# Two attentions and a gate on one core: the gate's path moved from DRAM to DVE, and the planner's rules for transfers changed

## The chip, the cores and the metric

The kernel runs on one core of a Trainium2 chip. The metric is device time in microseconds, less being better: the median of several runs. A profiled execution is one more run, and the profile's span goes from its first to its last instruction. Engines: TensorE (PE, its weight loads PEld), VectorE (DVE), ScalarE (ACT), GpSimd (POOL) and SyncE (SP), whose queue issues all transfers here.

## The reference

For 2048 tokens of width 640 there are two attentions of 32 heads (20 channels each), A and B, mixed by a gate that each token computes:

```python
g = sigmoid((x * gate_w).sum(-1, keepdims=True))
a = A(x, wq, wk, wv, wo, beta)      # 4 segments of 512 tokens
b = B(x, wqkv, wo)                  # causal window of 256 tokens
return g * a + (1 - g) * b
```

A is causal softmax attention within a segment, plus a memory: `num = phi(q) @ M`, `den = phi(q) @ z`, with `M` and `z` summed over `phi(k)` and `v` of the earlier segments, where `phi(t)` is `t + 1` for positive t and else `exp(t)`. A head's sigmoid of `beta` mixes `num / den` with the softmax part. Inputs and outputs are float32.

## The kernel before, in words

**Tiling.** The work is cut into 16 head groups `T` (four segments s, and in each of them the groups g = 0, 2, 1, 3 of `head(T)`; g below 2 is A, from 2 on B), and each of these into four units `u` of four heads, 64 in all. For a head group the projections run first: five column tiles `m` of q and k (`plan_qk`, matmuls of L432), and four token blocks of v (`plan_v`, L553). They are float32 products made of three matmuls on high and low halves, so each weight tile is loaded (`wst`, `xst`), split by ACT (L381) and by POOL or DVE (L397) into `w` or `wv`, and then used. q and k are split into three bfloat16 parts (`plan_parts`), stored to DRAM (`dq`, `dk`, by `qk_store`) and read back as stacks `qst`, `kst`, one set for each unit (`stack_read`). Likewise phi goes to `dphi` and `dphq` and comes back (`mem_load` into `pks`, `mem_stack` into `qfs`).

**A unit.** It first finds the maximum of each row: matmuls into PSUM (`max_mm`, L644), a reduction on DVE (`max_red`, L655), splits and a transpose (`mrs`, `mt`), two stores to DRAM (`max_store`, L682) and a read of three rows into the unit's own `qst` (`max_rows`, L686). Only then may the scores be computed, with the maximum subtracted in the same matmul (`st_mm`, L709), then the exponential on ACT (L716), masks on POOL (L722, L725), and the product with v (`av_mm`, L739). The result is scaled, transposed and stored (`o_store`), read back for the output projection (`o_load`, L432 with `ohl`) and stored.

**The gate.** The v projection of head group g = 0 has one more column, `gate_w`. `z_out` (L562) copies it to `zg`, one column for each of the segment's four token blocks. `z_store` (L566) writes these 4 x 128 values to DRAM (`dz`), single floats apart, and `z_load` (L570) reads them back into `zc` in the layout of the transposed output, repeated for four groups of 32 partitions. `z_exp` (ACT, L574) and `z_sig` (DVE, L578 to L580) make the sigmoid and one minus it. `fac` and `den_mul` scale by them later.

**What sets the order.** The kernel is written as a list of items: `add(t, engine, duration, function, ...)` with a due time `t` in units, the buffers that it makes (`new`), adds to (`put`), changes (`mod`) or reads (`get`), and for a transfer its size. `Plan.order` then plays a list scheduler: among the items whose dependencies are met it takes the one that can start first, by the due time's order on a tie, and the result is the order in which each engine's instructions are issued. It holds a model of 16 DMA rings: a transfer of `took` us per ring begins when its rings are free and lands `DM` us after them. What the model says of times decides only the order; on the chip the semaphores decide when things run. The tables at the head set due times: `AHEAD` (projections before their units), `RD` (reads of the stacks), `MT` and `MS` (maxima and what follows them), `PACE` (how far a projection may run ahead of the scores).

Of the kernel before, what the change touches and what calls it, by code (L numbers as in the profile page):

```python
# [37 lines left out]
NPX, NMI, NOB = 7, 2, 2  # L38
AHEAD, RD, PACE = 4.26, 2.5, 2.18
TL, OZ, WL = 1.16, 5, 0.006  # L40
P0, MA, DP, NF, NR = 3.97, 0.94, 0.0, 1, 2
MT, MS = 1.3, 0.58
WARM = 26
LM, LR, LA, AT = 0.99, 2.03, 0.0, 0.11
DM, XP, XO, XS = 0.9, 0.32, 0.2, 0.11
OA = {5: 2, 6: 3, 7: 2, 8: 2, 9: 2, 10: 2, 11: 3, 12: 3, 13: 2, 14: 2, 15: 2}
AV = ((0, 1, 2),)
EPS = 1e-6

# [5 lines left out]
class Plan:  # L55
# [38 lines left out]
    def order(self):  # L94
# [7 lines left out]
        for i, (t, _, eng, dur, fn, a, new, mod, put, get, size, pace, cols, _, bank, _, _) in enumerate(items):  # L102
# [48 lines left out]
            for name in get:  # L151
                s = slot(name)
                deps[i] |= set(s["puts"])
# [26 lines left out]
        while len(out) < n:  # L180
            best = None
            for e, c in cand.items():
                cold = e == "pe" and self.cold(free[e])
                for i in c:
                    at = free[e]
                    if e == "pe":
                        at += max(0.0, items[i][13][0] - tail)
                    z = max(at, ready[i]) + (items[i][15] if tail > 0.06 else 0.0)
                    if items[i][16] and e in ("dve", "pool"):
                        z = max(z, port)  # L190
                    if items[i][14]:
# [69 lines left out]
@with_exitstack  # L261
def gated_mix_kernel(ctx: ExitStack, tc: tile.TileContext, xt, wqk, wv, wo, beta, ident, out):
# [6 lines left out]
    attention(ctx, tc, const, dram, xt, wqk, wv, wo, beta, ident, o_dram, out)  # L269


def attention(ctx, tc, const, dram, xt, wqk, wv, wo, beta, ident, o_dram, out):
    nc = tc.nc
# [17 lines left out]

    idf = const.tile([128, 128], F32, name="idf")

    mask_a = const.tile([128, 512], BF16, name="mask_a")
# [60 lines left out]
    zg = const.tile([128, 16], F32, name="zg")  # L355
    dz = [dram.tile([L], F32, name=f"dz{i}") for i in range(NSEG)]
    zc = const.tile([128, 2, 2, 16], F32, name="zc")
# [166 lines left out]
    def plan_qk(t, dt, T, m):  # L524
# [3 lines left out]
        t += NC * dt - 0.01  # L528
        ph, dk = ("phi", T, m), ("dq", T)
        plan_parts(t + 1e-4, k, k)  # L530
        add(t + 3e-4, SP, SI * len(runs_of(m)), qk_store, T, m, put=[dk], get=[("hl", k)], size=3 * 2 ** 17, packet=1024)
        nk = rows_of(m, 1) if g < 2 and s < NSEG - 1 else 0
# [5 lines left out]
        if nk:  # L538
            add(t + 7e-4, SP, SI * len(runs_of(m, (1,))), phi_store, T, m, get=[ph],
                new=[("dphi", 2, ("dphi", T))] if m == 1 else [], put=[("dphi", T)] if m > 1 else [], size=2048 * nk)  # L540
        if nq:
            plan_parts(t + 8e-4, ph, ph)
            add(t + 1e-3, SP, SI * len(runs_of(m, (0,))), phl_store, T, m, get=[("hl", ph)],
                new=[("dphq", 2, ("dphq", T))] if m == 0 else [], put=[("dphq", T)] if m else [], size=3072 * nq, packet=1024)

# [18 lines left out]

    def z_store(s):
        nc.sync.dma_start(bass.AP(tensor=dz[s].tensor, offset=dz[s].offset, ap=[[1, 4], [16, 32], [4, 4]]),  # L566
                          zg[:, 4 * s:4 * s + 4])

    def z_load(s):
        nc.sync.dma_start(zc[:, s % 2, 0], bass.AP(tensor=dz[s].tensor, offset=dz[s].offset,  # L570
                                                   ap=[[0, 4], [16, 32], [1, 16]]))

    def z_exp(s):
        nc.scalar.activation(zc[:, s % 2, 0], zc[:, s % 2, 0], AF.Exp, scale=-1.0)  # L574

    def z_sig(s):
        z = zc[:, s % 2, 0]
        nc.vector.tensor_scalar(z, z, 1.0, None, op0=ALU.add)  # L578
        nc.vector.reciprocal(z, z)
        nc.vector.tensor_scalar(zc[:, s % 2, 1], z, -1.0, 1.0, op0=ALU.mult, op1=ALU.add)  # L580

# [5 lines left out]
    def plan_v(t, dt, T, b):  # L587
# [8 lines left out]
        if g == 0:  # L596
            add(t + 1e-4, DVE, 0.08, z_out, T, b, get=[k], put=["zg"])
            if b == 3:
                add(t + 2e-4, SP, DI, z_store, s, get=["zg"], put=[("dz", s)], size=2048, packet=4)
                add(t + 3e-4, SP, DJ, z_load, s, get=[("dz", s)], new=[("z", 2, ("z", s))], size=8192, packet=64, rings=4)  # L600
                add(t + 4e-4, ACT, 0.25, z_exp, s, mod=[("z", s)])
                add(t + 5e-4, DVE, 0.7, z_sig, s, mod=[("z", s)])

# [340 lines left out]
    add(-25, PE, 0.107 * WARM, c_warm, bank=("warm", 1, "warm"), cols=256 * WARM)  # L944
    add(-16.5, SP, 1.1, c_load, put=["cl"], size=2 ** 16)
    add(-3, ACT, 0.25, c_exp, get=["cl"], put=["ce"])
# [5 lines left out]
    for T in range(NT + 2):  # L952
# [38 lines left out]
        for u in range(4 * T, 4 * T + 4):  # L991
            tr = u - RD
            for i in range(3):
                for w in range(2):
# [16 lines left out]
    for u in range(NU):  # L1011
# [91 lines left out]
def layout(A_x, A_wq, A_wk, A_wv, A_wo, A_beta, B_x, B_wqkv, B_wo, gate_w):  # L1103
# [16 lines left out]
    def turn(w):  # L1120
        return w.reshape(NC, 128, NC, 128).transpose(2, 1, 0, 3).reshape(NC, 128, D)
    return dict(xt=n(n(A_x)[0].T), wqk=n(np.stack([turn(w) for w in qk])), wv=n(np.stack(vv)),
                wo=n(np.stack([turn(w) for w in (n(A_wo)[rows], n(B_wo)[rows], n(B_wo))])),
                beta=n(n(A_beta).reshape(8, 4).T), ident=np.eye(128, dtype=np.float32))

# [14 lines left out]
```

## Time and profile before

| | |
|---|---|
| runs (3) | 1178.53 us median, 1175.38 to 1179.56 |
| the profiled execution | 1183.04 us, its span 1181.3 us |
| mean granted TensorE clock | 0.979 |
| PE busy | 1093.2 us, 93% |
| DVE, ACT, POOL busy | 66%, 60%, 69% |
| transfers | 224.24 MB, mean 190 GB/s |

The profile is read like this: a group's line gives engine, operation, output<-input and shape, then busy time, mean duration and the idle time before it with what ended it (`<-`). A wait's row names who waited, for whom, the sum, the count and the longest, in us. A row of the chain that ended last gives its start, its length and what filled it; where that is a transfer, it runs from the issue to the landing. `SPq` is the queue that issues transfers. Names of buffers are those of the kernel, without numbers.

### The profile page before, as it was taken

To read this page: it belongs to the slowest core of one execution; us is meant where nothing else is said; L and a number is where in the kernel's file an instruction comes from. 1 tells how busy PE (TensorE), PEld (TensorE's weight loads), DVE (VectorE), ACT (ScalarE), POOL (GpSimd) and SP (SyncE) were. 2 spreads that over 40 slices of the span, in tenths; PEclk is the share of its full clock that TensorE was granted. 3 is DMA by queue.
4 is the path that set the end of the run, shared out by engine and by line. 5 is a ranking of instruction groups with operands and counts; after the bars stand their busy time and mean duration, and the time that the engine had idled before them with its cause. 6 is when DMAs were issued, how large, how long until landed. Compare 5 with 4: busy or idle time off the path is not lost.

```text
span 1181.3 us, 25003 instructions
## 1 busy us (share of the span) xinstructions
PE 1093.2 (93%) x8322; PEld 718.9 (61%) x8322; DVE 778.6 (66%) x2640; ACT 704.6 (60%) x1496; POOL 816.1 (69%) x1063
## 2 busy tenths in 40 slices
PE   9789999997999999989798999997979899999996
PEld 7565666664556666656465666665646557665564
DVE  3477887665768667976666866676647577567711
ACT  6246756675467755567454776646636477645661
POOL 9436674786568776688655877667757587756874
PEclk9989999998999999999899999999999999999999
DMA  6868878778887599777787868887588676788423
GB/s 212 171 180 195 220 195 206 186 192 183 218 204 197 143 210 253 200 193 219 160 219 188 204 167 220 209 209 178 156 171 223 172 206 160 220 202 216 137 91 107
DMA packets 194753, 224.24 MB, mean 190 GB/s; under 512 B 80768, under 2 KB 143616, under 8 KB 194624
## 3 DMA queue, kind: packets, MB, share of 16 engines
q1 hardware_dynamic: 194624, 222.64, 73.9%
q8 instruction: 66, 1.08, 0.4%
q14 instruction: 63, 0.52, 0.2%
HBM read 157.62 MB, written 64.95 MB: 188 GB/s over the span
## 4 chain that ended last, share of the span: by engine, by line
PE 52%; DMA 29%; DVE 6%; POOL 5%; ACT 3%; SPq 3%; issue 2%; POOLq 0%; DVEq 0%; ACTq 0%
PE bank L432 19%; PE bank L709 9%; PE bank L553 8%; PE bank L739 8%; PE bank L644 8%; DMA qst<-dmx 5%; DMA dmx<-mt 5%; DMA qst<-dq 4%; DMA xst<-wv 3%; DMA kst<-dk 3%; DVE bank L655 3%; DMA wst<-wqk 2%; DMA xst<-o_dram 2%; ACT P L716 1%; DMA pks<-dphi 1%
## 5 line engine op out<-in xcount | busy, mean ns | idle before, releaser
L716 ACT ACTIVATE P<-bank 128x512 f32<-128x512 f32 (+2 forms) x768 | 374.1, 559 | 121.6 <-PE bank L709 101.2
L432 PE MATMUL bank<-xhl,w 128*128 128x512 f32 x1200 | 363.8, 429 | 1.4 <-DVE xhl L397 0.4
L655 DVE CUSTOM_DVE_ANT_0 bank<-bank,mask_b 128x384 f32<-128x384 f32 (+2 forms) x512 | 260.2, 549 | 65.0 <-PE bank L644 63.9
L644 PE MATMUL bank<-kst,qst 120*128 120x384 bf16 (+3 forms) x1024 | 258.9, 314 | 33.8 <-DVE mx L655 12.8
L655 DVE CUSTOM_DVE_ANT_0 bank<-bank,mask_a 128x128 f32<-128x128 f32 (+3 forms) x512 | 238.2, 511 | 74.9 <-PE bank L644 73.6
L709 PE MATMUL bank<-qst,kst 123*128 123x384 bf16 (+2 forms) x1216 | 231.8, 293 | 38.6 <-DMA qst<-dmx 29.8
L397 POOL TENSOR_TENSOR w<-wst,w 128x640 fp32r<-128x640 f32 x119 | 185.4, 1558 | 92.5 <-ACT w L381 92.2
L432 PEld LDWEIGHTS bank<-xhl,w 128*128 128x128 f32 x1200 | 218.9, 192 | 46.1 <-issue 1.9
L722 POOL TENSOR_SCALAR_AFFINE_SELECT P<-P 128x512 f32<-128x512 f32 x256 | 161.0, 636 | 86.1 <-ACT P L716 80.2
L553 PE MATMUL bank<-wv,xhl 128*128 128x320 f32 (+1 forms) x960 | 194.9, 337 | 0.7 <-POOL wv L397 0.2
L432 PE MATMUL bank<-ohl,w 128*128 128x512 f32 x600 | 178.8, 425 | 6.5 <-POOL w L397 2.7
L709 PEld LDWEIGHTS <-kst 123*128 123x128 bf16 x1216 | 91.9, 99 | 142.3 <-issue 70.8
L644 PEld LDWEIGHTS <-qst 120*128 120x128 bf16 x1024 | 82.9, 99 | 131.1 <-issue 94.6
L739 PE MATMUL bank<-P,vau 128*32 128x384 f32 (+3 forms) x2432 | 159.9, 407 | 1.2 <-DVE mt L789 0.8
L553 PEld LDWEIGHTS bank<-wv,xhl 128*128 128x128 f32 x960 | 153.7, 192 | 11.4 <-DVE mx L655 1.4
L655 DVE DVE_READ_ACCUMULATOR2_ANT mx<- 128x1 f32 x1024 | 143.2, 140 | 0.0
L451 POOL TENSOR_TENSOR hl<-res,hl 128x512 bf16<-128x512 f32 x104 | 121.1, 1166 | 23.7 <-ACT hl L381 19.9
L820 DVE STREAM_TRANSPOSE ot<-bank 128x512 f32<-128x512 f32 x88 | 62.7, 713 | 108.5 <-PE bank L739 98.1
L432 PEld LDWEIGHTS bank<-ohl,w 128*128 128x128 f32 x600 | 109.4, 191 | 31.9 <-POOL ohl L397 4.6
L739 PEld LDWEIGHTS bank<-P,vau 128*32 128x32 f32 x2432 | 69.0, 109 | 82.3 <-issue 66.4
L381 ACT ACTIVATE w<-wst 128x640 fp32r<-128x640 f32 x121 | 89.5, 741 | 40.8 <-PE bank L432 16.3
L397 POOL TENSOR_TENSOR wv<-xst,wv 128x322 fp32r<-128x322 f32 x79 | 68.6, 878 | 48.6 <-ACT wv L381 46.7
(73 smaller groups left out, 907.9 us busy)
## 6 DMA issues: line engine op xcount, KB each, us to landing
wst<-wqk SPq DMA_DIRECT2D x80, 320.0 KB
o_dram<-ot SPq DMA_DIRECT2D x64, 256.0 KB
qst<-dq SPq DMA_DIRECT2D x64, 240.0 KB
kst<-dk SPq DMA_DIRECT2D x64, 240.0 KB
wst<-wo SPq DMA_DIRECT2D x41, 320.0 KB
xst<-wv SPq DMA_DIRECT2D x80, 161.0 KB
qst<-dq SPq DMA_DIRECT2D x64, 192.0 KB
xst<-o_dram SPq DMA_DIRECT2D x35, 256.0 KB
```

The costliest lines, as they stand in the source:

```text
L381: nc.scalar.activation(dst, src, AF.Copy)
L397: EN[e].tensor_tensor(out=t[:, 1], in0=B.pop(src), in1=f(t[:, 0]), op=ALU.subtract)
L432: nc.tensor.matmul(p, w[:, a, col:col + 128], x[:, b], start=(c == 0 and i == 0), stop=(c == NC - 1 and i == 2))
L451: EN[e].tensor_tensor(out=t[:, LO], in0=B["res", k], in1=t[:, MI], op=ALU.subtract)
L553: nc.tensor.matmul(p[:, :n], x[:, a, 128 * b:128 * b + 128], w[:, bb, :n], start=(c == 0 and i == 0), stop=(c == NC - 1 and i == 2))
L644: nc.tensor.matmul(pt[:, :n], qst[u % NQ][0:6 * DH, h, 128 * b:128 * b + 128], keys(u, 6 * DH, h, c0, n), start=True, stop=True)
L655: nc.vector.tensor_tensor_reduce(out=x, in0=x, in1=mk, scale=1.0, scalar=BIG, op0=ALU.add, op1=ALU.max, accum_out=B["M", u][:, j:j + 1])
L709: nc.tensor.matmul(pt[:, c:c + 128 * n], keys(u, 6 * DH + 3, h, c0, 128), q[0:6 * DH + 3, h, 128 * q0:128 * (q0 + n)], start=True, stop=True)
L716: nc.scalar.activation(B["P", u, b][:, 2 * p + r, c0:c1], B["st", u, b, p, r][:, c0:c1], AF.Exp, scale=SCALE)
L722: nc.gpsimd.affine_select(out=v, in_=v, pattern=[[0, 4], [1, 128]], compare_op=ALU.is_ge, fill=0.0, base=0, channel_multiplier=-1)
L739: nc.tensor.matmul(o[32 * j:32 * j + 32, 128 * q0:128 * (q0 + n)], v[:, VA * h:VA * h + 32], t[:, j, c:c + 128 * n], start=(b == 0 and i = ...
L820: nc.vector.transpose(B["ot", u][:, i].rearrange("p b e -> p (b e)"), B["o" if i == 0 else "num", u])
```

## The change

Five things:

- The gate no longer goes through DRAM. `z_move` copies `zg` by DVE, for each of four groups of 32 partitions, into the first 32 partitions of `zc`; exponential and sigmoid run on 32 partitions, and three more copies repeat the result.
- In the planner a transfer that takes more than `BULK` = 0.3 us on a ring is not planned to start until its rings have less than `BACK` = 3 us of work left. The maxima's stores and reads are shorter than that.
- `DM`, the planned time from the end of a transfer to its landing, is 1.5 instead of 0.9; the due times of projections, stacks and maxima are earlier (`AHEAD` 4.7, `RD` 2.9, `MT` 1.5, `MS` 0.78), and `PACE` is 2.6.
- Units 0 and 1 of a head group wait for the first half of q, k and phi, units 2 and 3 for the second, where each waited for what was declared of the whole.
- An identity matrix that nothing used is no longer loaded.

```diff
-AHEAD, RD, PACE = 4.26, 2.5, 2.18
+AHEAD, RD, PACE = 4.7, 2.9, 2.6
-MT, MS = 1.3, 0.58
+MT, MS = 1.5, 0.78
-DM, XP, XO, XS = 0.9, 0.32, 0.2, 0.11
+DM, XP, XO, XS = 1.5, 0.32, 0.2, 0.11
+BACK, BULK = 3, 0.3
...
+                    if items[i][10] and items[i][10][0] > BULK:
+                        z = max(z, max(dma[:items[i][10][1]]) - BACK)
...
     def c_load():
-        nc.sync.dma_start(idf, ident)
...
+        def halves(tag, kind):
+            first = lambda du: min(z for z in range(NC) for r in runs_of(z, (kind,)) if r[0] == du)
+            du = sorted({z[0] for z in runs_of(m, (kind,))})
+            return dict(new=[((tag, z), 2, (tag, T, z)) for z in du if first(z) == m],
+                        put=[(tag, T, z) for z in du if first(z) != m])
...
-    def z_store(s):
-        nc.sync.dma_start(bass.AP(tensor=dz[s].tensor, offset=dz[s].offset, ap=[[1, 4], [16, 32], [4, 4]]),
-                          zg[:, 4 * s:4 * s + 4])
-
-    def z_load(s):
-        nc.sync.dma_start(zc[:, s % 2, 0], bass.AP(tensor=dz[s].tensor, offset=dz[s].offset,
-                                                   ap=[[0, 4], [16, 32], [1, 16]]))
+    def z_move(s):
+        v = zc[0:32, s % 2, 0].rearrange("p (b j) -> p b j", j=4)
+        for j in range(4):
+            nc.vector.tensor_copy(v[:, :, j], zg[32 * j:32 * j + 32, 4 * s:4 * s + 4])
...
+        for h in range(1, 4):
+            nc.vector.tensor_copy(zc[32 * h:32 * h + 32, s % 2], z)
...
-                add(t + 2e-4, SP, DI, z_store, s, get=["zg"], put=[("dz", s)], size=2048, packet=4)
-                add(t + 3e-4, SP, DJ, z_load, s, get=[("dz", s)], new=[("z", 2, ("z", s))], size=8192, packet=64, rings=4)
+                add(t + 2e-4, DVE, 0.4, z_move, s, get=["zg"], new=[("z", 2, ("z", s))])
...
-                        get=[("dq", T)] + ([("dq", T - NSG)] if w and back(T) else []) +
+                        get=[("dq", T, u % 4 // 2)] + ([("dq", T - NSG, u % 4 // 2)] if w and back(T) else []) +
...
-                    add(u + 0.3 + 0.001 * i, SP, DI, mem_stack, u, i, get=[("dphq", T)],
+                    add(u + 0.3 + 0.001 * i, SP, DI, mem_stack, u, i, get=[("dphq", T, g // 2)],
...
-                    add(u - 0.3 + 0.001 * i, SP, DI, mem_load, u, i, get=[("dphi", T), "im"],
+                    add(u - 0.3 + 0.001 * i, SP, DI, mem_load, u, i, get=[("dphi", T, g // 2), "im"],
```

The order of nearly all instructions on every engine moves. Three places show it.

On SP, where head group 0 of the second segment is projected: before, from the maxima's second store (`dmx<-mt`) to the read of their rows (`qst<-dmx`), with the gate's store and, further on, its load:

```order
L682 DMA dmx<-mt 4x32x32
L566 DMA dz_121<-zg 4x128x1
L389 DMA xst<-wv 128x322 x2
L389 DMA wst<-wo 128x640
L487 DMA dq_106<-hl 96x3x512
L487 DMA dk_110<-hl 32x3x512
L860 DMA o_dram_63<-ot 128x512
L686 DMA qst_94<-dmx 3x2048
L506 DMA dphq_116<-hl 96x3x512
L748 DMA pks<-dphi_114 20x16x32 x4
L570 DMA zc<-dz_121 128x1x16
```

The same place after the change:

```order
L687 DMA dmx<-mt 4x32x32
L389 DMA wst<-wqk 128x640
L865 DMA o_dram_63<-ot 128x512
L389 DMA xst<-wv 128x322 x2
L389 DMA wst<-wo 128x640
L487 DMA dk_109<-hl 128x3x512
L691 DMA qst_93<-dmx 3x2048
L878 DMA xst<-o_dram_62 128x1x512
L753 DMA pks<-dphi_113 20x16x32
```

The gate's two transfers are gone; between the store and the read of the maxima there are six long transfers in both.

On DVE, where the gate of the last segment is made: before, from a reduction of maxima (`ISA bank,mx`) on:

```order
L655 ISA bank,mx<-bank,mask_a 128x384
L655 ISA mx 128x1
L820 STREAM_TRANSPOSE ot<-bank 128x512
L578 TENSOR_SCALAR zc<-zc 128x16
L579 RECIPROCAL zc<-zc 128x16
L580 TENSOR_SCALAR zc<-zc 128x16
```

After, from the copy out of the v projection (`zg<-bank`) on:

```order
L569 COPY zg<-bank 128x1
L575 COPY zc<-zg 32x4 x4
L582 TENSOR_SCALAR zc<-zc 32x16
L583 RECIPROCAL zc<-zc 32x16
L584 TENSOR_SCALAR zc<-zc 32x16
L586 COPY zc<-zc 32x32 x3
L681 STREAM_TRANSPOSE mt<-mrs_97 128x64
```

The sigmoid, which needs ACT's exponential of the copies, now follows them with nothing in between. So it does in the third segment; in the second one reduction stands between, in the first a transpose of `pks`.

On PE, for the last unit: before, the end of what lies between its last maximum and its first scores (`qst_94`):

```order
L432 MATMUL bank<-ohl,w 128x512 x9
L739 MATMUL bank<-P,vau_97 32x384 x4
L739 MATMUL bank<-P,vau_97 32x128 x4
L739 MATMUL bank<-P,vau_97 32x384 x4
L739 MATMUL bank<-P,vau_97 32x128 x4
L739 MATMUL bank<-P,vau_97 32x256 x8
L709 LDWEIGHTS kst_90
L709 MATMUL bank<-qst_94,kst_90 128x384
```

After, with the same unit's scores on `qst_93`:

```order
L432 MATMUL bank<-ohl,w 128x512 x15
L744 MATMUL bank<-P,vau_96 32x384 x4
L744 MATMUL bank<-P,vau_96 32x128 x4
L744 MATMUL bank<-P,vau_96 32x384 x4
L744 MATMUL bank<-P,vau_96 32x128 x4
L744 MATMUL bank<-P,vau_96 32x256 x8
L714 LDWEIGHTS kst_89
L714 MATMUL bank<-qst_93,kst_89 128x384
```

In that whole stretch stood 15 matmuls of an output projection (`ohl`) before and stand 24 now.

More of the change, by code (lines that the diff above doesn't have):

```diff
@@ L152, in order @@
                 s = slot(name)
+                assert s["puts"] or s["base"] is not None, (fn, a, name)
                 deps[i] |= set(s["puts"])
@@ L261, in gated_mix_kernel @@
 @with_exitstack
-def gated_mix_kernel(ctx: ExitStack, tc: tile.TileContext, xt, wqk, wv, wo, beta, ident, out):
+def gated_mix_kernel(ctx: ExitStack, tc: tile.TileContext, xt, wqk, wv, wo, beta, out):
     nc = tc.nc
@@ L268, in gated_mix_kernel, with attention @@
     o_dram = [dram.tile([H, 32, S], F32, name=f"o_dram{i}") for i in range(2)]
-    attention(ctx, tc, const, dram, xt, wqk, wv, wo, beta, ident, o_dram, out)
-def attention(ctx, tc, const, dram, xt, wqk, wv, wo, beta, ident, o_dram, out):
+    attention(ctx, tc, const, dram, xt, wqk, wv, wo, beta, o_dram, out)
+def attention(ctx, tc, const, dram, xt, wqk, wv, wo, beta, o_dram, out):
     nc = tc.nc
@@ L290, in c_warm @@
             nc.tensor.matmul(p[:, 0:256], ones[:, 0:128], ones, start=True, stop=True)
-    idf = const.tile([128, 128], F32, name="idf")
     mask_a = const.tile([128, 512], BF16, name="mask_a")
@@ L355, in attention @@
     zg = const.tile([128, 16], F32, name="zg")
-    dz = [dram.tile([L], F32, name=f"dz{i}") for i in range(NSEG)]
     zc = const.tile([128, 2, 2, 16], F32, name="zc")
@@ L528, in plan_qk @@
         t += NC * dt - 0.01
-        ph, dk = ("phi", T, m), ("dq", T)
+        ph = ("phi", T, m)
+        def halves(tag, kind):
[3 more added lines that the diff above has]
+                        put=[(tag, T, z) for z in du if first(z) != m])
         plan_parts(t + 1e-4, k, k)
-        add(t + 3e-4, SP, SI * len(runs_of(m)), qk_store, T, m, put=[dk], get=[("hl", k)], size=3 * 2 ** 17, packet=1024)
+        add(t + 3e-4, SP, SI * len(runs_of(m)), qk_store, T, m, put=[("dq", T, z) for z in sorted({z[0] for z in runs_of(m)})], get=[("hl", k)], size=3 * 2 ** 17, packet=1024)
         nk = rows_of(m, 1) if g < 2 and s < NSEG - 1 else 0
@@ L539, in plan_qk @@
             add(t + 7e-4, SP, SI * len(runs_of(m, (1,))), phi_store, T, m, get=[ph],
-                new=[("dphi", 2, ("dphi", T))] if m == 1 else [], put=[("dphi", T)] if m > 1 else [], size=2048 * nk)
+                size=2048 * nk, **halves("dphi", 1))
         if nq:
@@ L543, in plan_qk @@
             add(t + 1e-3, SP, SI * len(runs_of(m, (0,))), phl_store, T, m, get=[("hl", ph)],
-                new=[("dphq", 2, ("dphq", T))] if m == 0 else [], put=[("dphq", T)] if m else [], size=3072 * nq, packet=1024)
+                size=3072 * nq, packet=1024, **halves("dphq", 0))
     def v_mm(T, b, c):
@@ L562, in z_out @@
         nc.vector.tensor_copy(zg[:, 4 * s + b:4 * s + b + 1], B["v", T, b][:, 16 * DH:16 * DH + 1])
-    def z_store(s):
-        nc.sync.dma_start(bass.AP(tensor=dz[s].tensor, offset=dz[s].offset, ap=[[1, 4], [16, 32], [4, 4]]),
-                          zg[:, 4 * s:4 * s + 4])
-    def z_load(s):
-        nc.sync.dma_start(zc[:, s % 2, 0], bass.AP(tensor=dz[s].tensor, offset=dz[s].offset,
-                                                   ap=[[0, 4], [16, 32], [1, 16]]))
+    def z_move(s):
+        v = zc[0:32, s % 2, 0].rearrange("p (b j) -> p b j", j=4)
+        for j in range(4):
+            nc.vector.tensor_copy(v[:, :, j], zg[32 * j:32 * j + 32, 4 * s:4 * s + 4])
     def z_exp(s):
-        nc.scalar.activation(zc[:, s % 2, 0], zc[:, s % 2, 0], AF.Exp, scale=-1.0)
+        nc.scalar.activation(zc[0:32, s % 2, 0], zc[0:32, s % 2, 0], AF.Exp, scale=-1.0)
     def z_sig(s):
[L577 to L580, printed above, removed]
+        z = zc[0:32, s % 2]
+        nc.vector.tensor_scalar(z[:, 0], z[:, 0], 1.0, None, op0=ALU.add)
+        nc.vector.reciprocal(z[:, 0], z[:, 0])
+        nc.vector.tensor_scalar(z[:, 1], z[:, 0], -1.0, 1.0, op0=ALU.mult, op1=ALU.add)
+        for h in range(1, 4):
+            nc.vector.tensor_copy(zc[32 * h:32 * h + 32, s % 2], z)
     def va(T, b):
@@ L598, in plan_v @@
             if b == 3:
-                add(t + 2e-4, SP, DI, z_store, s, get=["zg"], put=[("dz", s)], size=2048, packet=4)
-                add(t + 3e-4, SP, DJ, z_load, s, get=[("dz", s)], new=[("z", 2, ("z", s))], size=8192, packet=64, rings=4)
+                add(t + 2e-4, DVE, 0.4, z_move, s, get=["zg"], new=[("z", 2, ("z", s))])
                 add(t + 4e-4, ACT, 0.25, z_exp, s, mod=[("z", s)])
-                add(t + 5e-4, DVE, 0.7, z_sig, s, mod=[("z", s)])
+                add(t + 5e-4, DVE, 0.9, z_sig, s, mod=[("z", s)])
     RUNS = (((0, 3 * DH), (3, DH), (4, 2 * DH + 8)), ((0, 2 * DH), (2, 3 * DH), (5, DH)))
@@ L944, in attention @@
     add(-25, PE, 0.107 * WARM, c_warm, bank=("warm", 1, "warm"), cols=256 * WARM)
-    add(-16.5, SP, 1.1, c_load, put=["cl"], size=2 ** 16)
+    add(-16.5, SP, DI, c_load, put=["cl"], size=2 ** 12, packet=32)
     add(-3, ACT, 0.25, c_exp, get=["cl"], put=["ce"])
@@ L1123, in layout @@
                 wo=n(np.stack([turn(w) for w in (n(A_wo)[rows], n(B_wo)[rows], n(B_wo))])),
-                beta=n(n(A_beta).reshape(8, 4).T), ident=np.eye(128, dtype=np.float32))
+                beta=n(n(A_beta).reshape(8, 4).T))
 def kernel(**inputs):
```

## The prediction

> **What bounds the kernel now.** I read the page first, then the waits of TensorE, then the time around the longest of them, on PE and on the DMA queue.
>
> ```profile
> span 1181.3 us, 25003 instructions
> PE 1093.2 (93%) x8322; PEld 718.9 (61%) x8322; DVE 778.6 (66%) x2640; ACT 704.6 (60%) x1496; POOL 816.1 (69%) x1063
> PEclk9989999998999999999899999999999999999999
> ```
>
> TensorE bounds it: it is busy for 1093.2 of 1181.3 us, so all other engines together can give at most the 88 us in which it stands idle, and what it loses where the granted clock is low (the 8s in the last row). The waits of PE, longest sums first, with count and longest one:
>
> ```profile
> PE bank L709 <- DMA qst<-dmx: 29.8, 13, 7.9
> PE bank L644 <- DVE mx L655: 12.8, 12, 8.3
> PE bank L644 <- ACT P L716: 8.2, 5, 5.3
> PE bank L644 <- DMA kst<-dk: 6.6, 4, 1.9
> PE bank L432 <- POOL w L397: 3.1, 4, 1.5
> ```
>
> Three different releasers have one or two very long waits each. In the timeline of PE these are four places (in brackets the idle time before the row):
>
> ```profile
> 62.28 0.91 PE L644 MATMUL bank<-kst,qst 120*128 120x384 bf16 x2 [8.28 <-DVE mx L655]
> 282.38 0.82 PE L709 MATMUL bank<-qst,kst 123*128 123x384 bf16 x2 [7.94 <-DMA qst<-dmx]
> 578.09 0.69 PE L644 MATMUL bank<-kst,qst 120*128 120x256 bf16 x2 [5.31 <-ACT P L716]
> 883.74 0.61 PE L709 MATMUL bank<-qst,kst 123*128 123x512 bf16 x1 [6.88 <-DMA qst<-dmx]
> ```
>
> Together 8.28 + 7.94 + 5.31 + 6.88 = 28.4 us, a third of all idle time, at the places where head group 0 of a new segment is projected. There the gate goes to DRAM and back (L566, L570). The timeline of the DMA queue has its four stores, and the chain that ended last has, right behind each, its four longest transfers; the fifth longest is the last row:
>
> ```profile
> 42.31 0.56 SPq L566 DMA_DIRECT2D dz<-zg  x1
> 265.13 0.53 SPq L566 DMA_DIRECT2D dz<-zg  x1
> 562.80 0.54 SPq L566 DMA_DIRECT2D dz<-zg  x1
> 868.30 0.52 SPq L566 DMA_DIRECT2D dz<-zg  x1
> ...
> 46.78 12.30 DMA wst<-wqk
> 271.33 11.00 DMA qst<-dmx
> 565.09 11.97 DMA xst<-wv
> 868.88 9.95 DMA dmx<-mt
> ...
> 34.24 8.01 DMA kst<-dk
> ```
>
> Four transfers of four kinds take 10 to 12 us each, and all were issued within 6.2 us after a store of the gate. At the second place the queue itself waits for that store:
>
> ```profile
> SPq L506 <- DMA dz<-zg: 5.8, 1, 5.8
> ...
> dz<-zg SPq DMA_DIRECT2D x4, 2.0 KB
> ...
> 277.88 0.31 SPq L506 DMA_DIRECT2D dphq<-hl  x1
> ```
>
> The store issued at 265.13 released its follower at 277.88: 2 KB took over 12 us. It writes 512 floats one by one, and what stands behind it in the rings lands only after it: the small read at 271.33 landed at 282.33, and PE started at 282.38. At 62 and 578 the late transfers are the projections' weights, which hold ACT, and DVE and PE behind it:
>
> ```profile
> 577.09 0.47 ACT L381 ACTIVATE wv<-xst 128x322 fp32r<-128x322 f32 x1 [7.06 <-DMA xst<-wv]
> ```
>
> Each stall is followed by a stretch of half clock (columns: us, then busy time with instructions of PE, PEld, DVE, ACT, POOL, then granted clock, DMA share, GB/s):
>
> ```profile
> 56.00:66.20 10.20, 3.92 (x14) 3.11 (x14) 4.39 (x19) 3.69 (x8) 4.57 (x5) 0.50 0.87 252
> 277.90:288.10 10.20, 5.72 (x19) 3.31 (x20) 4.49 (x12) 5.30 (x12) 7.28 (x11) 0.50 0.87 255
> 574.80:581.60 6.80, 3.51 (x9) 2.09 (x8) 2.48 (x6) 4.43 (x12) 3.96 (x5) 0.50 0.80 190
> 882.00:888.80 6.80, 5.06 (x14) 2.74 (x15) 1.90 (x9) 3.00 (x9) 2.33 (x4) 0.50 0.84 216
> sum 34.00, PE 18.21 PEld 11.26 DVE 13.26 ACT 16.42 POOL 18.14; mean PE 4.55 PEld 2.81 DVE 3.31 ACT 4.11 POOL 4.54
> ```
>
> PE worked for 18.21 us at half clock there, which full clock does in half: 9.1 us lost.
>
> **The change, part by part.** The sum is made against the profiled execution, 1183.0 us (span 1181.3); the median of the runs, 1178.5, is 4.5 us lower, and I take the same difference off it.
>
> *The gate's way (store and load out, copies on DVE in).* Without the four stores the four stalls and their half clock go: 28.4 + 9.1 = 37.5 us. What is late next there:
>
> ```profile
> 635.11 0.60 PE L709 MATMUL bank<-qst,kst 123*128 123x512 bf16 x2 [3.56 <-DMA qst<-dmx]
> ```
>
> The other waits for the small read are 29.8 - 7.94 - 6.88 = 15.0 us in 11 places, 1.4 us each. At the second place the new order still has six bulk transfers between the last store of the maxima and their read, as the section on the change shows, so I leave such a wait at each of the four places, +5.5 us (bounds: 0, and four times the longest other wait of the kind, the row above: 14.2).
>
> What is added, per segment: four copies of 32x4 and three of 32x32 on DVE.
>
> ```profile
> L562 DVE COPY zg<-bank x16: 147/151/159, 26.8 to 868.1; 128x1 f32<-128x1 f32 x16
> L574 ACT ACTIVATE zc<-zc x4: 199/212/224, 64.3 to 885.8; 128x16 f32<-128x16 f32 x4
> DVE zc L578 <- ACT zc L574: 8.4, 1, 8.4
> ```
>
> At 0.15 us (first row, the nearest copy) 7 x 4 x 0.15 = 4.2 us of DVE, which is busy 66%; its idle third covers that, and uncovered it would be 4.2 us. New is where DVE stands: in three of the four segments the sigmoid comes right behind the copies or one reduction later, so DVE waits for the exponential on ACT and whatever ACT has ahead of it. Between 0.2 us (the exponential alone) and 8.4 us (the one such wait in the trace, itself behind a store); behind it wait the reductions of the maxima, and PE for their banks: 12.8 - 8.3 = 4.5 us in 11 other waits, 0.4 each. I take 4 x 0.4 = +1.6 us, nearest to the low end because without the store nothing but compute is ahead; the high end stays as a rival. POOL gets no new instruction, and SP issues two DMAs fewer per segment.
>
> *Later landings, the hold-back of bulk transfers, earlier due times, waits by halves.* These change no instruction, only the order, so one price for all. They aim at the 15.0 us of waits for the small read and the 6.6 us for k: 21.6 us. At the last unit 24 matmuls of an output projection stand between its last maximum and its first score where 15 stood. A matmul of that shape costs 0.27 us by two rows:
>
> ```profile
> 570.09 1.76 PE L432 MATMUL bank<-xhl,w 128*128 128x512 f32 x6
> 571.84 0.94 PE L432 MATMUL bank<-xhl,w 128*128 128x512 f32 x3
> 1131.51 0.83 PE L709 MATMUL bank<-qst,kst 123*128 123x384 bf16 x6 [1.58 <-DMA qst<-dmx]
> ```
>
> (1.76 - 0.94) / 3 = 0.27, nine more are 2.5 us, and the wait of 1.58 us there would be covered. Elsewhere the spacing moved both ways, so I take a third of 21.6: -7 us, bounds -21.6 (all gone) and +7 (as much new). At the start the order of the queue changes as well; I price that with the rest.
>
> ```profile
> idf<-ident SPq DMA_DIRECT2D x1, 64.0 KB
> L381 ACT ACTIVATE w<-wst 128x640 fp32r<-128x640 f32 x121 | 89.5, 741 | 40.8 <-PE bank L432 16.3
> ```
>
> *The identity's load* goes from the start: 64 KB (first row) at 252 GB/s, as the first of the half-clock stretches moved them, is 0.26 us, hidden behind the loads around it; 0. The other row is wanted below.
>
> Sum: -37.5 + 5.5 + 1.6 - 7 = -37.4 us; 1183.0 - 37.4 = 1145.6 for a profiled execution, 1178.5 - 37.4 = 1141.1 for the median. I say 1141.
>
> **The rivals.**
> - *More is won.* If the later landings cover nearly all of the 21.6 us and nothing takes the stalls' place, -37.5 - 20 + 1.6 = -55.9: 1122.6. For it: the waits on DMA are spread thin (1.4 us), so a little more distance covers many. Against it: distance given to one unit is taken from another.
> - *The stores are innocent.* The long transfers also stand where weights, q, k and o are issued together; then the stalls stay, and with them the time: 1178.5 less the 7 of the new order, plus the 1.6 of DVE, 1173. Against it: 34.24 with 8.01 us is the longest piece without such a store. [...]
> - *A wait in its place.* DVE stands at the sigmoid for 8.4 us in each segment, as it did once: 4 x 8.4 = 33.6 us of the 37.5 come back, 1141 + 33.6 - 1.6 = 1173; at two of the four places, 1157.
> - *Slower: weights held back.* Holding bulk transfers until the queues are short can bring the weights late; 121 weight tiles pass (the w row above). It decides from 37.4 / 121 = 0.3 us per tile on; at 0.4 us each, +48 us: 1189. For it: POOL's w already makes PE wait. Against it: 3.1 us in 4 waits is all there is in 121 tiles. [...]
>
> **How the numbers follow.** The forecast 0.62; more won 0.20; innocent 0.05; a wait in its place 0.09; slower 0.04. The forecast's own range is 1126 to 1158: below by the 14.6 us of the 21.6 that the sum leaves in place; above by 8.7 (the four waits for the small read at their upper bound) and 8.0 (one wait of DVE at 8.4 instead of 0.4). The range for 8 in 10 reaches to most of the second case and the half-way form of the fourth: 1118 to 1162. The runs shown lie within 0.36% of each other, so 0.5% (5.9 us) is about what can be told from no change: faster, below 1172.6: 0.62 + 0.20 + 0.09 x 0.7 + 0.05 x 0.4 = 0.90, and same takes nearly all the rest of those two: 0.05; slower 0.05.
>
> **What would show it.** Right: no PE wait over 4 us and none of 5 us near a segment's first projection; the waits for the small read at 8 to 15 us instead of 29.8; no transfer of the chain over 9 us; half clock under 20 us in all; the wait of DVE at the sigmoid under 2 us each. Wrong: stalls of 5 to 8 us at the same four places (stores innocent), DVE idle before the sigmoid with PE waiting for L655's successor (a wait in its place), or waits of the projections for POOL's w of 10 us and more (weights held back).

## The result, and the profile after

| | before | after |
|---|---|---|
| median in the same job | 1176.95 us (1168.55 to 1179.56) | 1116.9 us (1115.24 to 1118.56) |
| ratio | 1 | 0.9501, 95% interval 0.945 to 0.9553 |
| span of the profiled execution | 1181.3 us | 1113.5 us |
| PE busy | 1093.2 us, 93% | 1075.5 us, 97% |
| span minus PE busy | 88.1 us | 38.0 us |
| mean granted TensorE clock | 0.979 | 0.997 |

The change takes 60 us off, where I had said 37; 1116.9 lies 1.1 us below my range. The page of the kernel after (span, engines, and the granted clock over 40 slices):

```profile
span 1113.5 us, 25006 instructions
PE 1075.5 (97%) x8322; PEld 714.2 (64%) x8322; DVE 784.1 (70%) x2661; ACT 703.6 (63%) x1503; POOL 815.6 (73%) x1063
PEclk9999999999999999999999999999999999999999
```

The number of matmuls is the same, 8322, and none of the 8s in the clock's row is left. The waits of PE in the kernel after (sum, count, longest):

```profile
PE bank L714 <- DMA qst<-dmx: 4.4, 8, 1.0
PE bank L432 <- POOL w L397: 3.5, 4, 1.5
PE bank L649 <- DMA kst<-dk: 3.1, 2, 1.8
PE bank L714 <- DVE mx L660: 3.1, 2, 2.5
PE bank L649 <- DVE ot L825: 2.5, 1, 2.5
...
PE bank L649 <- ACT P L721: 1.4, 4, 0.6
PE bank L649 <- DVE mx L660: 1.4, 4, 0.5
```

The longest wait is 2.5 us, where there had been four of 5.3 to 8.3 us. The waits for the small read of the maxima fell from 29.8 to 4.4 us in sum, those of the maxima's matmuls for the reductions (L660, L655 before) from 12.8 to 1.4. The gate on DVE, after: what DVE waited for at the sigmoid, and then, from the view of the tile `zc`, the copies (minimum, median and maximum in ns, first and last start):

```profile
DVE zc L582 <- ACT zc L578: 0.6, 2, 0.3
```

```profile
L575 DVE COPY zc<-zg x16: 158/182/1109, 36.6 to 814.3; 32x4 f32<-32x4 f32 x16
L586 DVE COPY zc<-zc x12: 170/173/807, 40.3 to 816.8; 32x32 f32<-32x32 f32 x12
```

The two longest transfers in the chain that ended last of the kernel after:

```profile
327.56 9.10 DMA qst<-dq
739.86 9.11 DMA xst<-xt
```

Both are far from a segment's first projection, where 10 to 12 us had been spent.

For what follows, each span is split into three: span minus PE busy (idle); what PE lost at half clock, put at half of its busy time inside the stretches with a granted clock of 0.50 (in the kernel after, 9 matmuls of 128x512 fill the 3.41 us from 1096.11 on at 0.50, and 16 the 3.37 us from 1099.53 on at 1.00); and the rest, PE's work as if at full clock. Before: 88.1 + 15.7 + 1077.5 us. After: 38.0 + 3.4 + 1072.1. So of the 67.8 us between the spans 50.1 are idle time, 12.3 half clock, and 5.4 are in the rest, which varies between 1072 and 1080 us from kernel to kernel; matmul ends are modelled, and I have no cause for that part.

### The profile page after: what moved, and what is told of

Same layout as the page of the kernel before. It is cut to its first block, busy times and chain, and to the rows that moved or that the text cites. A ratio compares the mean times of both kernels' runs of the same rounds, so it can differ in the third digit from the quotient of the medians.

```text
span 1113.5 us, 25006 instructions
## 1 busy us (share of the span) xinstructions
PE 1075.5 (97%) x8322; PEld 714.2 (64%) x8322; DVE 784.1 (70%) x2661; ACT 703.6 (63%) x1503; POOL 815.6 (73%) x1063
## 4 chain that ended last, share of the span: by engine, by line
PE 73%; DMA 14%; DVE 5%; POOL 3%; SPq 2%; issue 1%; ACT 1%; POOLq 0%; DVEq 0%; ACTq 0%
PE bank L432 27%; PE bank L744 12%; PE bank L714 11%; PE bank L649 11%; PE bank L560 11%; DMA qst<-dq 3%; DMA qst<-dmx 3%; DMA kst<-dk 2%; DMA dmx<-mt 2%; DMA xst<-xt 1%; DVE bank L660 1%; DMA xst<-o_dram 1%; SPq L624 1%; POOL w L397 1%; DMA qfs<-dphq 1%
## 5 line engine op out<-in xcount | busy, mean ns | idle before, releaser
L432 PE MATMUL bank<-xhl,w 128*128 128x512 f32 x1200 | 358.3, 426 | 3.3 <-POOL w L397 1.8
L660 DVE CUSTOM_DVE_ANT_0 bank<-bank,mask_b 128x384 f32<-128x384 f32 (+2 forms) x512 | 259.6, 554 | 35.8 <-PE bank L649 35.2
L660 DVE CUSTOM_DVE_ANT_0 bank<-bank,mask_a 128x128 f32<-128x128 f32 (+3 forms) x512 | 239.1, 512 | 52.2 <-PE bank L649 51.1
L432 PEld LDWEIGHTS bank<-xhl,w 128*128 128x128 f32 x1200 | 218.0, 190 | 47.6 <-POOL w L397 2.9
L714 PE MATMUL bank<-qst,kst 123*128 123x384 bf16 (+2 forms) x1216 | 229.4, 288 | 12.8 <-DMA qst<-dmx 4.4
L560 PE MATMUL bank<-wv,xhl 128*128 128x320 f32 (+1 forms) x960 | 198.0, 339 | 0.4 <-DVE mx L660 0.2
L432 PE MATMUL bank<-ohl,w 128*128 128x512 f32 x600 | 179.8, 426 | 5.6 <-POOL ohl L397 2.2
L649 PEld LDWEIGHTS <-qst 120*128 120x128 bf16 x1024 | 83.6, 98 | 103.4 <-issue 67.8
L660 DVE DVE_READ_ACCUMULATOR2_ANT mx<- 128x1 f32 x1024 | 145.8, 142 | 0.0
L451 POOL TENSOR_TENSOR hl<-res,hl 128x512 bf16<-128x512 f32 x104 | 121.1, 1165 | 15.7 <-ACT hl L381 15.0
L432 PEld LDWEIGHTS bank<-ohl,w 128*128 128x128 f32 x600 | 109.2, 191 | 28.3 <-POOL ohl L397 4.1
L381 ACT ACTIVATE w<-wst 128x640 fp32r<-128x640 f32 x121 | 90.3, 747 | 29.8 <-PE bank L432 15.2
L381 ACT ACTIVATE hl<-res 128x512 bf16<-128x512 f32 x104 | 66.5, 639 | 37.8 <-DVE res L444 18.6
```

The source lines that it names most:

```text
L381: nc.scalar.activation(dst, src, AF.Copy)
L432: nc.tensor.matmul(p, w[:, a, col:col + 128], x[:, b], start=(c == 0 and i == 0), stop=(c == NC - 1 and i == 2))
L451: EN[e].tensor_tensor(out=t[:, LO], in0=B["res", k], in1=t[:, MI], op=ALU.subtract)
L560: nc.tensor.matmul(p[:, :n], x[:, a, 128 * b:128 * b + 128], w[:, bb, :n], start=(c == 0 and i == 0), stop=(c == NC - 1 and i == 2))
L649: nc.tensor.matmul(pt[:, :n], qst[u % NQ][0:6 * DH, h, 128 * b:128 * b + 128], keys(u, 6 * DH, h, c0, n), start=True, stop=True)
L660: nc.vector.tensor_tensor_reduce(out=x, in0=x, in1=mk, scale=1.0, scalar=BIG, op0=ALU.add, op1=ALU.max, accum_out=B["M", u][:, j:j + 1])
```

## The experiments

The first theory is that of the prediction: the gate's store of 512 single floats holds up what is issued behind it, and the planner's rules matter little. Its rivals are that the store is innocent, and that the planner's rules carry the gain. Times are medians; the ratio is to the kernel before in the same job, over all runs, so it is not quite the quotient of the medians; the last three columns split the span of the one profiled execution as above. The kernel after was timed in the first job only, and before differs by 3.4 us between the jobs (1175.04 to 1178.41 us), so a difference to after of that size says nothing.

| run | us | ratio, 95% interval | span | idle | lost at half clock | rest |
|---|---|---|---|---|---|---|
| before | 1176.95 | 1 | 1181.3 | 88.1 | 15.7 | 1077.5 |
| e1_store_rows | 1143.71 | 0.9737, 0.970 to 0.9775 | 1146.5 | 53.7 | 16.2 | 1076.6 |
| e2_gate_dve_same_order | 1142.48 | 0.9731, 0.9681 to 0.9781 | 1140.8 | 48.6 | 16.0 | 1076.1 |
| e4_after_extra_store | 1144.66 | 0.9743, 0.9708 to 0.9778 | 1141.3 | 56.2 | 12.5 | 1072.6 |
| e5_gate_only | 1150.77 | 0.9796, 0.9758 to 0.9834 | 1147.6 | 60.4 | 10.2 | 1076.9 |
| e8_after_due | 1143.45 | 0.9722, 0.9688 to 0.9756 | 1144.8 | 54.0 | 12.5 | 1078.3 |
| e7_after_dm | 1131.92 | 0.9612, 0.9568 to 0.9656 | 1129.9 | 48.0 | 10.2 | 1071.8 |
| e9_after_no_halves | 1127.1 | 0.9569, 0.9529 to 0.9609 | 1126.5 | 43.6 | 8.5 | 1074.4 |
| e6_after_no_hold | 1122.56 | 0.9547, 0.9507 to 0.9587 | 1122.5 | 38.9 | 5.0 | 1078.5 |
| e11_after_old_projections | 1122.13 | 0.954, 0.9479 to 0.960 | 1121.2 | 38.1 | 3.4 | 1079.7 |
| e13_further | 1121.08 | 0.9548, 0.9482 to 0.9615 | 1119.5 | 36.9 | 9.7 | 1072.8 |
| e12_after_dm_152 | 1120.95 | 0.9552, 0.9492 to 0.9611 | 1119.7 | 37.2 | 10.1 | 1072.4 |
| e10_after_old_maxima | 1117.32 | 0.9507, 0.945 to 0.9563 | 1116.9 | 33.5 | 9.4 | 1074.1 |
| after | 1116.9 | 0.9501, 0.945 to 0.9553 | 1113.5 | 38.0 | 3.4 | 1072.1 |

### The gate's store alone

e1 is the kernel before, in the same order, with the store's DRAM layout changed: 128 runs of 16 bytes instead of 512 single floats. The gate's values then arrive in another layout, so tokens are mixed with gates that are not theirs; only the time is of use here.

```diff
-        nc.sync.dma_start(bass.AP(tensor=dz[s].tensor, offset=dz[s].offset, ap=[[1, 4], [16, 32], [4, 4]]),
+        nc.sync.dma_start(bass.AP(tensor=dz[s].tensor, offset=dz[s].offset, ap=[[4, 128], [1, 4]]),
                           zg[:, 4 * s:4 * s + 4])
```

> The kernel before, every engine's order unchanged; only the gate's store writes each partition's four values as one run of 16 bytes (128 runs) instead of 512 single floats, so the gate's values arrive in another layout. If the 512 single floats hold the rings (theory), the four stalls of 5 to 8 us and their half clock go and the time falls by some 37 us, to about 1140. If a store of 2 KB is cheap and the stalls come from the bulk transfers around it or from the order (rival), it stays at 1177, within 5 us.

Measured: 1143.71 us, 33 us less than before. The waits of PE and the longest transfer of the chain in e1:

```profile
PE bank L709 <- DMA qst<-dmx: 13.8, 11, 3.7
PE bank L644 <- DVE mx L655: 5.5, 13, 0.9
```

```profile
602.66 8.99 DMA qst<-dmx
```

One line of one transfer's shape, 2 KB four times, is worth over half of the change. The stores are not innocent, and it is neither their bytes nor the round trip through DRAM that costs, since e1 keeps both; it is the way in which the 2 KB are written. e1 changes three things of it at once: the number of writes (128 for 512), their size (16 bytes for 4) and the order of the access pattern, with which their share among the rings may change too. Which of these costs the time, no run here separates.

### The gate on DVE, in the order of before

e2 puts the copies of the change where the load stood, drops the store, and leaves the order of everything else.

```diff
     def z_store(s):
-        nc.sync.dma_start(bass.AP(...), zg[:, 4 * s:4 * s + 4])
+        pass
     def z_load(s):
-        nc.sync.dma_start(zc[:, s % 2, 0], bass.AP(...))
+        v = zc[0:32, s % 2, 0].rearrange("p (b j) -> p b j", j=4)
+        for j in range(4):
+            nc.vector.tensor_copy(v[:, :, j], zg[32 * j:32 * j + 32, 4 * s:4 * s + 4])
```

> The kernel before with its order of items, but the gate's store is left out and the copies by DVE stand where the gate's load stood; sigmoid on 32 partitions and three more copies as after. Theory: as with 16-byte runs, 1140 or a few us less, since store and load are both gone. Rival (the order won the time): 1177. If DVE's wait for the exponential eats the gain: 1157 to 1173, with waits of several us at the sigmoid.

Measured: 1142.48 us, 34 us less than before and the same as e1 within the intervals. The page's head and the waits of PE in e2:

```profile
span 1140.8 us, 25019 instructions
PE 1092.2 (96%) x8322; PEld 719.7 (63%) x8322; DVE 789.8 (69%) x2668; ACT 703.0 (62%) x1496; POOL 816.2 (72%) x1063
```

```profile
PE bank L711 <- DMA qst<-dmx: 8.0, 7, 1.9
PE bank L646 <- DVE mx L657: 6.5, 13, 1.2
PE bank L711 <- DVE mx L657: 5.5, 8, 1.6
PE bank L646 <- DMA kst<-dk: 3.4, 4, 2.3
```

No long wait is left, the copies cost nothing that can be seen, and DVE has no wait at the sigmoid at all. But PE is as busy as before (1092.2 against 1093.2 us): in the profiled execution the idle time fell by 39.5 us, and what is lost at half clock not at all.

### The store put back into the kernel after

e4 is the kernel after, with the old store issued again beside the copies; nothing reads what it writes, and the order is else the same.

```diff
             nc.vector.tensor_copy(v[:, :, j], zg[32 * j:32 * j + 32, 4 * s:4 * s + 4])
+        nc.sync.dma_start(bass.AP(tensor=dz[s].tensor, offset=dz[s].offset, ap=[[1, 4], [16, 32], [4, 4]]),
+                          zg[:, 4 * s:4 * s + 4])
```

> The changed kernel with all engines' order unchanged and the old store of 512 single floats issued besides, once per segment right after the copies; nothing reads it. Theory: the four stalls come back, 1117 + 20 to 38, so 1137 to 1155, with PE idle 5 to 8 us at each; at the low end if the wider spacing of the new order hides part of each 10 us. Rival: 1117 to 1120.

Measured: 1144.66 us, 27.8 us more than after. The four stores in the queue's timeline, three of the longest transfers of the chain, and the waits that came of them in PE's timeline, all of e4:

```profile
36.66 0.57 SPq L577 DMA_DIRECT2D dz<-zg  x1
266.21 0.56 SPq L577 DMA_DIRECT2D dz<-zg  x1
548.53 0.54 SPq L577 DMA_DIRECT2D dz<-zg  x1
834.12 0.53 SPq L577 DMA_DIRECT2D dz<-zg  x1
```

```profile
39.16 12.12 DMA qst<-dq
...
269.23 10.07 DMA dphq<-hl
...
836.98 11.09 DMA xst<-wv
```

```profile
51.49 0.58 PE L652 MATMUL bank<-kst,qst 120*128 120x128 bf16 x3 [6.89 <-DMA qst<-dq]
280.75 0.61 PE L652 MATMUL bank<-kst,qst 120*128 120x512 bf16 x2 [4.05 <-DMA o_dram<-ot]
559.62 0.38 PE L717 MATMUL bank<-qst,kst 123*128 123x384 bf16 x2 [2.57 <-ACT P L724]
844.27 0.38 PE L652 MATMUL bank<-kst,qst 120*128 120x512 bf16 x1 [2.07 <-issue]
849.10 1.01 PE L717 MATMUL bank<-qst,kst 123*128 123x256 bf16 x4 [3.53 <-ACT P L724]
```

Three times a transfer issued some 3 us behind a store takes 10 to 12 us, whatever its kind, and 10 to 15 us behind each store PE stands idle: 6.89 + 4.05 + 2.57 + 2.07 + 3.53 = 19.1 us in all, at two of the four places less than the 5 to 8 us that I expected. The split says the same: idle +18.2, half clock +9.1, rest +0.5. So the store costs 28 us with the new order as well as some 33 us with the old one; the two parts of the change overlap by a few us only.

### The gate alone, planned anew

e5 has the gate as the change has it, planned, with all other rules and numbers of before.

```diff
-                add(t + 2e-4, SP, DI, z_store, s, get=["zg"], put=[("dz", s)], size=2048, packet=4)
-                add(t + 3e-4, SP, DJ, z_load, s, get=[("dz", s)], new=[("z", 2, ("z", s))], size=8192, packet=64, rings=4)
+                add(t + 2e-4, DVE, 0.4, z_move, s, get=["zg"], new=[("z", 2, ("z", s))])
```

> The kernel before with only the gate's part of the change, planned as in the change (old due times, old landing time, no hold-back, no halves). Theory: 1140, so that some 23 us of the change's 60 are left for the planner's rules. If the gate is the whole of it: 1117. Rival: 1177.

Measured: 1150.77 us, 10.8 us more than expected and 8.3 us more than e2, which differs from it only in the order. From here to the kernel after it is 33.9 us, from e2 25.6: that is what the planner's rules brought, where I had put 7.

### One rule of the planner taken out at a time

Each of these is the kernel after with one rule undone and the whole planned anew.

```diff
# e6_after_no_hold
-                    if items[i][10] and items[i][10][0] > BULK:
-                        z = max(z, max(dma[:items[i][10][1]]) - BACK)
# e7_after_dm
-DM, XP, XO, XS = 1.5, 0.32, 0.2, 0.11
+DM, XP, XO, XS = 0.9, 0.32, 0.2, 0.11
# e8_after_due
-AHEAD, RD, PACE = 4.7, 2.9, 2.6
-MT, MS = 1.5, 0.78
+AHEAD, RD, PACE = 4.26, 2.5, 2.18
+MT, MS = 1.3, 0.58
# e9_after_no_halves: dq, dphi and dphq are declared and waited for whole, as before
-                        get=[("dq", T, u % 4 // 2)] + ([("dq", T - NSG, u % 4 // 2)] if w and back(T) else []) +
+                        get=[("dq", T)] + ([("dq", T - NSG)] if w and back(T) else []) +
```

> The changed kernel without the hold-back of bulk transfers. The gate alone left 26 to 34 us to the planner's rules. Theory P (the hold-back carries them, since small reads get ahead): 1135 to 1145, waits for the small read back to some 15 us. Rival Q (the later landing time or the earlier due times carry them): 1117 to 1125. Rival R (any replanning moves the time by some 8 us either way, no rule is decisive): within 8 us of 1117.

> The changed kernel with the planned landing 0.9 us after a transfer's end, as before, instead of 1.5. Theory P: 1117 to 1125. Rival Q with the landing time: 1135 to 1145, waits for the small read up from 4.4 to some 12 us, since each unit has two or three landings in its chain and so some 1.5 us less distance. Rival R: within 8 us of 1117.

> The changed kernel with the old due times and the old pace (AHEAD, RD, PACE, MT, MS as before). Theory P: 1117 to 1125. Rival Q with the due times: 1135 to 1145, with waits for q, k and the small read. Rival R: within 8 us of 1117.

> The changed kernel with waits for what was declared of the whole of q, k and phi, as before. All theories: within 8 us of 1117, since the stacks are read well after their stores in either order; if the halves matter, 1125 to 1140 with waits for kst and qst.

Measured, against 1116.9: without the hold-back +5.7 us, with the old `DM` +15.0, with all old due times +26.6, without the halves +10.2. The four add up to 57.5 us, while all rules together brought 26 to 34, so they don't add: with the old due times the other three rules bring nothing against e2 (1143.45 us, 1142.48 there) and 7.3 us against e5, which like e8 was planned anew. So theory P fell with e6. Theory Q holds for the due times; with the old `DM` the waits came as expected, but the time lies 3 us below the 1135 expected. The rows of PE's waits for the small read, in e7, and then in e8 with the one for q:

```profile
PE bank L714 <- DMA qst<-dmx: 16.6, 15, 2.7
```

```profile
PE bank L714 <- DMA qst<-dmx: 17.7, 11, 5.2
...
PE bank L649 <- DMA qst<-dq: 4.1, 2, 2.2
```

With either undone these waits are back, 16.6 and 17.7 us against 4.4. Without the hold-back they are not, as the same row of e6 shows:

```profile
PE bank L712 <- DMA qst<-dmx: 5.2, 5, 2.5
```

### Which due times, and how much of it is chance

e10 undoes the maxima's due times alone, e11 the projections', e13 goes as far again in the change's direction. e12 is a control: `DM` 1.52 instead of 1.5 says nothing that any theory could use, but it moves many instructions in the order of PE and of the queue.

```diff
# e10_after_old_maxima
+MT, MS = 1.3, 0.58
# e11_after_old_projections
+AHEAD, RD, PACE = 4.26, 2.5, 2.18
# e12_after_dm_152
+DM, XP, XO, XS = 1.52, 0.32, 0.2, 0.11
# e13_further
+AHEAD, RD, PACE = 5.0, 3.05, 2.9
+MT, MS = 1.65, 0.93
```

> The changed kernel with the old due times of the maxima (MT 1.3, MS 0.58). With all old due times it took 1143, with waits for the small read of 17.7 us. Theory M (the maxima's lead carries it): 1135 to 1143, those waits over 12 us. Rival N (the projections' and stacks' lead): 1117 to 1125, waits for the small read under 8 us.

> The changed kernel with the old due times of projections and stacks and the old pace (AHEAD 4.26, RD 2.5, PACE 2.18), the maxima's new ones. Theory M: 1117 to 1125. Rival N: 1135 to 1143. If both parts must move together (the stacks must be there before the maxima start): both this and the other one over 1130.

> The changed kernel with DM 1.52 instead of 1.5: a change without meaning, which still moves over a third of PE's and of the queue's rows. It measures what any replanning does. If the rules matter by their sense: 1117, within 4 us. Rival R (the order is a lottery): 8 us or more away, and the 5 to 15 us of single rules are then not theirs.

> The changed kernel with the due times moved as far again as the stacks' buffers allow (AHEAD 5.0, RD 3.05, PACE 2.9, MT 1.65, MS 0.93). If more lead still covers waits: 1108 to 1114. If the buffers (four stacks, three banks for maxima) already bind: 1117 to 1125.

Measured: e10 +0.4 us against after, e11 +5.2, e13 +4.2, and the control +4.1. The intervals of all four overlap that of after. So neither half of the due times carries the 26.6 us of e8: with either of them earlier nearly all is kept, and only with both old it is lost. Why one is enough stays open. In e10 the waits moved to another place, as its waits of PE show, with no net loss:

```profile
PE bank L649 <- DVE mx L660: 8.0, 10, 4.5
PE bank L714 <- DMA qst<-dmx: 6.1, 8, 1.9
```

The control sets the measure for all replanned kernels: an order that is different for no reason is 4 us off, and e5 against e2 gives 8. By that, `DM` (+15.0) and the due times (+26.6) go beyond what chance did here; the halves (+10.2) lie at the edge; the hold-back (+5.7) cannot be told from chance, and the intervals of both overlap that of after. Two things bear on how far that goes. Two orders are a small sample of chance, and after is the best of all kernels here: against the control the four rules are worth 11.0, 22.5, 6.2 and 1.6 us. And the waits for the small read, 16.6 and 17.7 us in e7 and e8, lie between 0.2 and 9.7 us in e6 and e9 to e13, control included, which speaks for `DM` and the due times by their sense. Of the halves it does not: in e9 PE has no wait for k and 1.5 us of waits for q, where such waits were expected if the halves matter. Going further (e13) brings nothing, and no run beat the kernel after: e10's 1117.32 is equal to it.

## Why the prediction was right, and where it was wrong

- **PE bounds it, and the four stalls come from the gate's stores: right.** Shown by taking only the single floats away (e1, -33 us), only the store (e2, -34), and by putting it back (e4, +28).
- **-37.5 us for stalls and their half clock: right in sum, wrong in parts.** With the residual waits and DVE the gate was to give -37.5 + 5.5 + 1.6 = -30.4 us; e2 gives -34.2. But in the order of before the half clock was not won: 15.7 us lost there before, 16.0 in e2, at other places. The idle time fell by more instead, 39.5 us rather than 28.4: beyond the four stalls the waits for the small read fell from 15.0 to 8.0 us and those for k from 6.6 to 3.4, while those for L655's reductions, without the stall of 8.3, rose from 4.5 to 6.5. That is read from one execution of each kernel. The granted clocks of all runs are 0.971 to 0.977 for before in that job, 0.985 in both profiled executions of e1 and e2, but 0.992 and 0.993 in e1's other runs and up to 0.996 in e2's; so over all runs some of the half clock was won.
- **+5.5 us of residual waits for the small read: wrong in sign.** No wait took the stalls' place. The 15.0 us that were there beside the two stalls became 8.0 in e2 and 4.4 after the whole change, below the 8 to 15 I had named.
- **+1.6 us of DVE standing at the sigmoid: too much.** It waited 0.6 us in all (the row of L582). The copies have medians of 0.18 and 0.17 us, but some took up to 1.1 us, and they sum to 6.9 + 2.7 = 9.6 us of DVE against my 4.2, with no wait of PE to show for it.
- **-7 us for the planner's rules: the step that failed.** They brought 25.6 us from e2 to after, more than my bound of 21.6. I priced only idle time, of two kinds of waits, and took a third of it. Between the spans of e2 and after are 27.3 us: 10.6 of idle time, 12.6 of half clock (16.0 to 3.4), 4.0 in the rest. So in these two executions the idle part was not far from my 7, and the half clock that came behind scattered waits of some 2 us (1.93 us at 917.69 in e2, shown further on) is what I left out, though the prediction had just charged it to the four stalls. Over all runs its part is smaller. The granted clocks are 0.985, 0.996, 0.988 and 0.985 in e2 and 0.997, 0.993, 0.997 and 0.997 after; PE lost 0.47 us per us of half clock in both profiles. As an estimate from these, half clock makes some 8 of the 26.5 us between the mean spans (1141.7 and 1115.2), and the e2 run at 0.996 still had a span of 1138.2 us. So the third that I took of the idle time was too little as well.
- **The hidden load of the identity at 0** was not tried by itself.
- **The rivals.** "More is won" (1122.6) came nearest, for another reason than it gave: it too counted only waits. "Stores are innocent" fell with e1. "A wait in its place" fell with the 0.6 us. "Weights held back" fell: PE's waits for POOL's `w` at L432 went from 3.1 to 3.5 us; and since e6 is 5.7 us slower than after, within what chance orders do, the hold-back is neither shown to help nor to harm.
- **What would show it.** No wait over 4 us: right, 2.5. No transfer over 9 us: missed by a hair, 9.10 and 9.11. Half clock under 20 us in all: right, inside the span the stretches sum to 7.2 us, from 50.1 before.

## What to carry to other kernels

A store whose runs are single elements is to be priced by what is issued behind it, not by its bytes alone: here transfers behind 2 KB as 512 writes of 4 bytes took 10 to 12 us, and with 128 writes of 16 bytes no transfer of the chain took more than 8.99. Look for transfers that take several times their usual length shortly behind such a store, and widen its runs first. Waits like those of 1.84 and 1.93 us here, on the bounding engine, are not to be priced by their sum alone; count the stretches of half clock that follow them. And before a rule of a scheduler is credited with a few microseconds, run a change of order that means nothing: here that alone was worth 4 to 8 us.

## What the runs showed of the hardware

*Half clock came behind waits of some 2 us as well as behind the long ones.* In the kernel before nine stretches with a granted clock of 0.50 lie inside the span, 50.1 us in all, and in the kernel after three: from 549.98 and from 1096.11 on for 3.4 us each, and the last 0.3 us. Two stretches of e2 (columns as in the prediction), then two of the kernel after with the same sort of wait, a little shorter:

```profile
915.60:919.00 3.40, 1.47 (x16) 0.75 (x13) 1.09 (x3) 0.88 (x2) 2.05 (x2) 1.00 0.76 232
919.00:922.40 3.40, 3.40 (x12) 2.08 (x10) 2.50 (x7) 2.30 (x5) 2.04 (x4) 0.50 1.11 199
```

```profile
764.96:768.37 3.41, 1.66 (x11) 1.37 (x11) 3.34 (x10) 2.11 (x5) 2.42 (x7) 1.00 0.41 118
768.37:771.78 3.41, 3.41 (x19) 2.51 (x18) 2.32 (x8) 2.12 (x4) 2.83 (x3) 1.00 0.38 89
```

In e2 PE was busy for 1.47 of 3.40 us, and 12 instructions filled the next 3.40 us at clock 0.50; after, 1.66 of 3.41 us, and 19 filled the next 3.41 us at 1.00. The wait behind the first, in PE's timeline of e2, is one of those for the small read:

```profile
917.69 0.83 PE L711 MATMUL bank<-qst,kst 123*128 123x384 bf16 x6 [1.93 <-DMA qst<-dmx]
```

So a wait of 1.93 us cost that and, as an estimate (half of the 3.40 us of busy time at 0.50), 1.7 us more. Half clock came at other places behind as much and behind less: PE idled for 1.84 of the 3.40 us from 546.60 on in the kernel after, all of it one wait for k, and the next 3.40 us ran at 0.50; so it was with 2.03 us of idle time from 1092.70 on there, 1.91 from 1079.50 on in e2, and 2.48 from 752.50 on in e12. In e2 it came behind 1.14 us of idle time in the 3.40 us from 290.90 on, and in the kernel after not behind the 1.75 us from 764.96 on, shown above. So in these traces the idle time alone does not tell where half clock comes; what else decides was not shown. The control has nearly the same idle time as after (37.2 and 38.0 us) and loses 10.1 us at half clock instead of 3.4; those 6.7 us are all of the 6.2 us between the spans, and why it loses more was not shown either.

*Behind a store of 2 KB transfers took 10 to 12 us.* In e4 nothing reads what the four stores write and nothing waits for them, yet three of the transfers issued behind them landed only after 12.12, 10.07 and 11.09 us. It does not look as if the 512 writes stood in line for all that time, as the prediction had it: in the kernel before 569, 713, 558 and 667 packets under 512 bytes, the stores' among them, are counted in the 5 us from the issue of each store on, and 15, 12, 17 and 24 in the next 5 us. But in the 8 us that begin 2.5 us behind each of these stores the DMA engines move 40, 45, 55 and 30 GB/s, where the mean of the span is 190. In e4 and e1 the 8 us that begin 2 us behind the last store are these:

```profile
836.10:844.10 8.00, 6.10 (x72) 3.75 (x65) 4.10 (x19) 3.66 (x11) 3.41 (x6) 1.00 0.35 36
```

```profile
846.80:854.80 8.00, 7.91 (x75) 4.55 (x73) 4.53 (x18) 2.84 (x6) 6.23 (x8) 1.00 0.81 181
```

They move 36 GB/s behind the single floats and 181 behind the runs of 16 bytes. What slows the transfers in those 8 us the records do not show.
